# Cluster attention and two soft mixtures on one core: small TensorE products padded to the whole array, centroid products moved behind the product with v

## Chip, cores, metric

One core of a Trainium2 chip runs one program. The metric is the device time in microseconds (us) of one execution; the kernel before takes 589.06 us in the median of three runs (588.84 to 589.12).

## What is computed

The program chains three blocks; the change lies in the first. For 2 x 8 heads of 768 positions and 64 channels:

```python
q_assign = argmax(q_n @ c_n.T)            # 16 centroids per head, q and c normalised
k_assign = argmax(k_n @ c_n.T)
mask = q_assign[:, None] == k_assign[None, :]
scores = where(mask, scale * q @ k.T, -1e9)
attn = softmax(scores)                     # sum + 1e-9
x = attn @ v                               # (1536, 512) over the heads
h = x @ w_in                               # 512 -> 2048, f64 words decoded on the chip
g = P(h) / (Q(h) + 1e-6)
x = g @ w_out                              # 2048 -> 512
out = soft_moe(x, phi, w1, w2)             # logits = x @ phi, 32 slots
```

`w_out @ phi` is formed ahead of time (the tile `wphi0`), so that the logits can be had straight from g.

## The kernel before

**Attention** works on eight pairs of heads. A pair takes twelve slots; slot n (n from 0 to 95, k = n % 12, loop at line 692) computes one 128-row tile of transposed scores for both heads (`a2_mm`, lines 458 and 459), its exponential on ScalarE (`a2_exp`, 463), and the product with v of the slot before (`a2_av`, 472). In the same slot, ten slots ahead (`LEAD`), runs the pass that finds row maxima and sums: `a1_mm` (383, 384) on TensorE, the negated copy with the row minimum on VectorE (`a1_neg`, 393), the exponential with the row sum on ScalarE (`a1_exp`, 401). Two PSUM tiles (`psS`) are shared: `a2_mm` waits for `a2_exp`, `a1_mm` for `a1_neg` of the slot before. `a1_neg` also follows `a1_exp` of the slot before, since both use the tile `nv`.

**Side work** is put into the slots by hand. A plan holds, for a slot, lists by engine; the order of PE, ACT, DVE and POOL is the order written (`manual_schedule`). A slot issues the lists S, A, D0, D, D1, D2, G0, G (DMA; ScalarE; VectorE; GpSimd), then `a2_mm`, `a2_exp`, `a2_av` of the slot before, `a1_exp`, `a1_mm`, `a1_neg`, and last the list P of TensorE (739). Three kinds of side work exist.

- `prep(p)` (236) readies a later pair, from k = 8 on, over 18 slots: two groups of centroid products (`scores`, 251, at k = 9 and 10), scaling (`scaled`, 256), transposes (`scT`, 266), the argmax on VectorE (`best`, `first`), one-hot transposes (`ohT`, 293, k = 3), their copy with row counts on ScalarE (`count`, 296, k = 4), the mask weights (`masks`, 304, k = 6), two products `nonhot` (309, k = 6), four products `alive` (322, k = 8 to 11), and GpSimd's splits of q and k into parts (260 to 335).
- `stats` (403) turns sums into a bias that enters the scores: GpSimd steps (419 to 432, k = 8 and 2 or a slot later), two transposes `rows` (437, k = 10 and 4) and two VectorE multiplies `place` (444, k = 11 and 5).
- `decode_steps` (551) turns the f64 words of w_in and w_out into floats: VectorE (563, 564, 570, 574), ScalarE (567), GpSimd (579, 586, 587). For w_out, `wphi_steps` (595) adds transposes (601), a product with phi (610), a copy (617), and after each fourth block transposes (622) and a reduction (625). One decode starts every third slot, from slot 72 on every second.

All small TensorE results go to a ring of three PSUM tiles (`m_tile`, 167), so a small product also waits until the reader of the third tile back is done. TensorE products here have these array shapes: scores of `a1` and `a2` and all f32 transposes use 128 columns and 80 or 128 rows; `scores` 64 rows x 32 columns, `alive` 64 x 128, `nonhot` 64 x 64, `ohT` 128 x 64, `rows` and the phi product 128 x 32, the product with v 128 x 64.

After attention (from about 335 us) come `h_mm` and the mixtures; the change doesn't touch them.

Of the kernel before, what the change touches and what calls it, by code (L numbers as in the profile page):

```python
# [8 lines left out]
F32 = mybir.dt.float32  # L9
F32R = mybir.dt.float32r  # L10
BF16 = mybir.dt.bfloat16
# [26 lines left out]
def shape_constants():  # L38
    c = np.zeros((128, C_END), np.float32)
    p = np.arange(128)  # L40
    c[p, C_ID + p] = 1.0
    c[:, C_SUM:C_SUM + 128] = p[:, None] % 32 == p[None, :] % 32
    c[0:32, C_SGN] = 1.0
    c[32:64, C_SGN] = -BIG

    for i in range(3):
        c[96 + 6 * i:99 + 6 * i, C_STAT + i] = 1.0
        c[99 + 6 * i:102 + 6 * i, C_STAT + i] = -1.0
    b = np.zeros((128, B_END), np.float32)
    b[p, B_ID + p] = 1.0  # L50

    b[0:16, B_MASK:B_MASK + 128] = 1.0
    b[16:32, B_MASK + 128:B_MASK + 256] = 1.0
    b[0:16, B_MASK + 256:B_MASK + 272] = 1.0
    b[16:32, B_MASK + 272:B_MASK + 288] = 1.0
    for i in range(64):
        b[i, B_ADD + 256 + i] = -1.0 if i < 32 else 1.0
    b[:, B_RANK:B_RANK + 16] = 16.0 - np.arange(16)
    return c, (b.view(np.uint32) >> 16).astype(np.uint16)
# [3 lines left out]
def tile_kernel(ctx, tc, qT, kT, v, cenT, cenP, consts, constsb, ab, w_in, w_out, phi, w1, w2, out, dbg=None):  # L63
# [22 lines left out]
    def xs_tile(dt, name):  # L86
# [42 lines left out]
    OPENW = 4  # L129
    ops = [[{n: att.tile([128, S], F32R, name=f"{n}_{i}_{h}") for n in ("q1", "q2", "k1", "k2")}  # L130
            for h in range(2)] for i in range(NBUF)]
    stat = [att.tile([128, 2, 32], BF16, name=f"stat{i}") for i in range(2)]
    for t in stat:
        POOL.memset(t, 0.0)

    def fill(i):
        for h in range(2):
# [34 lines left out]
    def first_pair(r, o, f):  # L172

        hold = f["hold"]

        def nonhot_k(h):
            m = psS.tile([128, 2, 512], F32, tag="S", name="s1")
            for c in range(2):
                PE.matmul(m[64:80, c, 0:HS], hold["W"][:, 288 + 16 * h:304 + 16 * h],
                          hold["oT"][:, c * HS:(c + 1) * HS], start=True, stop=True)  # L180
            ACT.activation(o[h]["k2"][64:80, :].rearrange("p (c n) -> p c n", c=2), m[64:80, :, 0:HS], AF.Copy, scale=-BIG)

        def nonhot_q(h, c):
            m = m_tile()
            w = slice(c * HS, (c + 1) * HS)
            PE.matmul(m[64:80, 0:HS], hold["W"][:, 256 + 16 * h:272 + 16 * h], hold["oT"][:, w], start=True, stop=True)
            ACT.copy(o[h]["q2"][64:80, w], m[64:80, 0:HS])

        def q0(h):
            w = slice(0, HS)  # L190
            q1, q2 = o[h]["q1"], o[h]["q2"]
            qa = hold.pop(("qa", h, 0))
            ACT.copy(q1[:, w], qa)
            POOL.tensor_scalar(q2[0:64, w], qa[0:64, :], 1.0, 1.0, ALU.mult, ALU.mult)
            DVE.tensor_tensor(q1[64:128, w], qa[64:128, :], q1[64:128, w].bitcast(F32), ALU.subtract)

        def front():
            f["scores"](0)
# [12 lines left out]
            idle(12)  # L211
            f["ohT"]()
            f["count"]()
            idle(8)
            f["masks"]()

        def back():
            f["alive"](0, 0)
            f["alive"](1, 0)
            f["qalive"](0, 0)  # L220
            f["qalive"](1, 0)
            nonhot_k(0)
            q0(0)
            nonhot_q(0, 0)
            q0(1)
            nonhot_k(1)
            nonhot_q(1, 0)
            idle(4)

        rest = [(0, "P", lambda: (f["alive"](0, 1), f["alive"](1, 1))),  # L230
                (1, "D", lambda: (f["qalive"](0, 1), f["qalive"](1, 1))),
                (1, "G", lambda: (f["qsplit"](0, 1), f["qsplit"](1, 1))),
                (1, "P", lambda: (nonhot_q(0, 1), nonhot_q(1, 1)))]
        return front, back, rest

    def prep(p):
# [52 lines left out]

        def ohT():  # L290
            m = hold["mo"] = m_tile(BF16)
            for i in range(6):
                PE.transpose(m[0:64, i * 128:(i + 1) * 128], hold["oh"][:, i].rearrange("p g c -> p (g c)"), identb)

        def count():
            ACT.activation(tile_(t_p, "oT", [64, S], BF16), hold.pop("mo")[0:64, 0:S], AF.Identity,
                           accum_out=tile_(s2_p, "cnt", [64, 1], F32))

        def masks():

            pres = tile_(s2_p, "pres", [64, 1], F32)
            DVE.memset(pres, 0.0)
            DVE.tensor_scalar(pres[0:32, :], hold["cnt"][32:64, :], 1.0, None, ALU.min)
            DVE.scalar_tensor_tensor(tile_(s2_p, "W", [64, B_ADD - B_MASK], BF16), cb[0:64, B_MASK:B_ADD], pres,
                                     cb[0:64, B_ADD:B_RANK], ALU.mult, ALU.add)

        def nonhot(c):
            m = hold["m", c] = m_tile()
            PE.matmul(m[0:64, 0:HS], hold["W"][:, 256:320], hold["oT"][:, c * HS:(c + 1) * HS], start=True, stop=True)

        def signed(c):
            nh = hold["nh"] if c else tile_(t_p, "nh", [64, S], F32R)
# [24 lines left out]
        if p == 0:  # L337
            return first_pair(r, o, locals())
        return [
            (1, "P", lambda: scores(0)),  # L340
            (2, "P", lambda: scores(1)),
            (3, "A", lambda: scaled(0)),
            (3, "P", lambda: scT(0)),
            (4, "A", lambda: scaled(1)),
# [58 lines left out]
    def stats(p, half):  # L403
# [8 lines left out]
        def parts(a):  # L412

            nv, ssum = nvs[p, half]
            l = hold["l"]
            st = stat[half][:, :, 0:18].rearrange("p h (i k r) -> p k h i r", i=3, k=2)
            val = nv.rearrange("p k (h i) -> p k h i", h=2)
            if a == 0:
                POOL.tensor_scalar(hold["s"], ssum, 1e-9, 1.0, ALU.add, ALU.mult)
# [13 lines left out]

        def rows():
            hold["m"] = m_tile(BF16)
            for h in range(2):
                PE.transpose(hold["m"][96:128, h * 128:(h + 1) * 128], stat[half][:, h, :], identb)

        def place():

            m = hold["m"]
            own = cst[96:128, C_STAT:C_END].unsqueeze(2).to_broadcast([32, 3, 128])
            for h in range(2):
                DVE.tensor_tensor(ops[p % NBUF][h]["q2"][96:128, half * HS:(half + 1) * HS].rearrange("p (i t) -> p i t", i=3),
                                  m[96:128, h * 128:(h + 1) * 128].unsqueeze(1).to_broadcast([32, 3, 128]), own, ALU.mult)

        return [(0, "A", log)] + [(0, "G0", lambda a=a: parts(a)) for a in range(6)] + [(1, "P", rows), (2, "D0", place)]

# [141 lines left out]
        return [(-3, "S", dma), (0, "D1", bits), (1, "A", expo), (1, "D1", mant), (2, "D1", sign),  # L590
                (3, "G0", value)] + (after(hold) if after else [(4, "G", parts)])

    wph = {}

    def wphi_steps(f):

        def steps(hold):
            def tr():
                m = hold["m"] = m_tile()
                for c in range(NCC):  # L600
                    PE.transpose(m[:, c * 128:(c + 1) * 128], hold["w"][:, c * 128:(c + 1) * 128], ident)

            def tcopy():
                hold["wT"] = dec_p.tile([128, 512], F32, tag="wT", name="wT")
                ACT.copy(hold["wT"], hold.pop("m"))

            def mm():
                m = hold["m"] = m_tile()
                for c in range(NCC):
                    PE.matmul(m[32 * c:32 * c + 32, 0:128], ph[:, c, :], hold["wT"][:, c * 128:(c + 1) * 128],  # L610
                              start=True, stop=True)

            def keep_():
                k = f % 4
                if k == 0:
                    wph["t"] = dec_p.tile([128, 512], F32, tag="wph", name="wph")
                DVE.tensor_copy(wph["t"][:, k * 128:(k + 1) * 128], hold.pop("m")[:, 0:128])

            def fin():
                m = hold["m"] = m_tile()  # L620
                for k in range(4):
                    PE.transpose(m[:, k * 128:(k + 1) * 128], wph["t"][:, k * 128:(k + 1) * 128], ident)

            def total():
                DVE.tensor_reduce(wphi0[:, f - 3:f + 1, :], hold.pop("m").rearrange("p (k c s) -> p k s c", k=4, c=4),
                                  AX.X, ALU.add)

            return [(4, "P", tr), (5, "A", tcopy), (5, "P", mm), (6, "D1", keep_)] + \
                ([(6, "P", fin), (7, "D1", total)] if f % 4 == 3 else [])
        return steps  # L630

    w_in_w = w_in.bitcast(I32)
# [59 lines left out]
    for n in range(-LEAD, NSL + 1):  # L692
# [25 lines left out]
        if n > 0:  # L718
            pp, pk = divmod(n - 1, 12)
            a2_av(pp, pk)  # L720
            if pk % 6 == 5:
                copy, split = a2_x(pp, pk // 6)
                copy()
                if n < NSL:
                    add(n + (1 if k else 2), [(0, "G", split)])
                else:
                    split()
# [465 lines left out]
```

## Time and profile before

| | |
|---|---|
| median of three runs | 589.06 us |
| span of the profiled execution, first to last instruction | 588.3 us |
| what the median holds beside that span | 0.8 us |
| busy in the span: PE, DVE, ACT, POOL | 553.0, 462.1, 392.4, 375.0 us |
| attention's slots 0 to 95 | 41 to 335 us |
| granted TensorE clock | 1.00 of full speed throughout attention |

Busy times of TensorE include pipelining, so 94% of the span doesn't mean that it never waits. L458 is line 458 of the kernel before. In a timeline a row is start, duration, engine, line, operation, output<-inputs, shapes, count and, in brackets, the idle time before it and what ended it; in the chain of waits a row is start, duration, engine, output and line.

### The profile page before, as it was taken

How to read it: one execution, taken by the hardware profiler on the slowest of the kernel's cores; microseconds unless marked ns; L12 is line 12 of the kernel's file. 1: busy time of each engine (PE TensorE's matmuls, PEld its weight loads, DVE VectorE, ACT ScalarE, POOL GpSimd, SP SyncE). 2: the span in 40 equal slices, each digit the busy share in tenths (PEclk: the TensorE clock that was granted, in tenths of full speed). 3: DMA queues.
4: the chain of work that ended last, by engine and by line, in shares of the span. 5: the costliest groups of instructions: out<-in, count | busy, mean ns of one | idle time of the engine just before them, and what ended most of it. 6: DMA issues, size and time to landing. Idle time of an engine off the chain costs nothing.

```text
span 588.3 us, 9927 instructions
## 1 busy us (share of the span) xinstructions
PE 553.0 (94%) x3345; PEld 343.3 (58%) x3348; DVE 462.1 (79%) x817; ACT 392.4 (67%) x713; POOL 375.0 (64%) x487
## 2 busy tenths in 40 slices
PE   8899999999999999999899999999999999988995
PEld 3455555565555555555555587777577767743363
DVE  5789788798788896888996179999989998971033
ACT  3577777677677776877777478878678876750111
POOL 8759899697996997979668375565456654611000
PEclk9999999999999999999999999999999999999999
DMA  8613553353434542333342476775476665379996
GB/s 224 218 60 118 166 195 125 115 197 139 143 117 166 197 150 91 114 132 124 128 159 90 144 247 222 269 251 211 159 283 229 227 230 191 121 321 364 421 418 255
DMA packets 37906, 113.77 MB, mean 193 GB/s; under 512 B 5216, under 2 KB 5664, under 8 KB 33248
## 3 DMA queue, kind: packets, MB, share of 16 engines
q1 hardware_dynamic: 37856, 113.14, 54.6%
q8 instruction: 26, 0.43, 0.3%
q14 instruction: 24, 0.20, 0.1%
HBM read 96.02 MB, written 15.73 MB: 190 GB/s over the span
## 4 chain that ended last, share of the span: by engine, by line
PE 56%; DVE 23%; ACT 8%; issue 6%; POOL 5%; DMA 2%; SPq 0%; DVEq 0%; POOLq 0%; ACTq 0%
PE h L809 6%; PE h L810 5%; PE h L812 5%; PE s L383 5%; DVE neg L393 5%; PE av L472 4%; PE s L458 4%; PE s L384 3%; PE s L459 3%; PE pb L1044 3%; PE pb L1115 3%; DVE mh L564 2%; ACT neg L401 2%; PE gt L870 2%; ACT e L463 2%
## 5 line engine op out<-in xcount | busy, mean ns | idle before, releaser
L393 DVE TENSOR_SCALAR_CACHE_REDUCE neg<-s 128x768 f32<-128x768 f32 x96 | 91.2, 952 | 36.6 <-ACT neg L401 25.7
L463 ACT ACTIVATE e<-s 128x768 f32<-128x768 f32 x96 | 77.5, 807 | 58.4 <-PE s L459 58.3
L401 ACT ACTIVATE neg<-neg,nv 128x768 f32<-128x768 f32 x96 | 89.5, 932 | 9.5 <-DVE neg L393 9.3
L383 PE MATMUL s<-k,q 128*128 128x384 f32 x192 | 75.7, 394 | 13.0 <-DVE neg L393 9.2
L840 POOL TENSOR_SCALAR q<-u,babs 128x512 f32<-128x512 f32 x47 | 39.6, 844 | 70.5 <-ACT u L838 70.5
L472 PE MATMUL av<-e,vt 128*64 128x384 f32 x384 | 83.2, 511 | 0.2 <-ACT e L463 0.2
L809 PE MATMUL h<-xh,w 128*128 128x512 f32 x192 | 80.6, 420 | 0.0
L383 PEld LDWEIGHTS s<-k,q 128*128 128x128 f32 x192 | 36.2, 189 | 68.1 <-DVE neg L393 27.4
L810 PE MATMUL h<-xl,w 128*128 128x512 f32 x192 | 75.9, 395 | 0.0
L458 PE MATMUL s<-q,k 128*128 128x384 f32 x192 | 73.2, 381 | 0.7 <-DVE neg L393 0.6
L842 POOL TENSOR_TENSOR q<-q,u 128x512 f32<-128x512 f32 x47 | 62.8, 1337 | 3.9
L384 PE MATMUL s<-k,q 80*128 80x384 f32 x192 | 65.0, 339 | 0.0
L459 PE MATMUL s<-q,k 128*128 128x384 f32 x192 | 64.7, 337 | 0.0
L812 PE MATMUL h<-xh,w 128*128 128x512 f32 x192 | 52.6, 396 | 0.0
L579 POOL TENSOR_TENSOR w<-mh,ex 128x512 f32<-128x512 f32 x32 | 44.1, 1378 | 10.8 <-DMA w_out<-w 5.4
L809 PEld LDWEIGHTS h<-xh,w 128*128 128x128 f32 x192 | 36.2, 189 | 16.1 <-issue 1.9
L458 PEld LDWEIGHTS s<-q,k 128*128 128x128 f32 x192 | 36.0, 188 | 16.2 <-issue 8.1
L849 ACT ACTIVATE r<-q,epsc 128x512 f32<-128x512 f32 (+1 forms) x49 | 33.5, 685 | 17.0 <-POOL q L842 16.4
L859 DVE SCALAR_TENSOR_TENSOR p<-q,p 128x512 f32<-128x512 f32 (+1 forms) x49 | 44.0, 901 | 0.1
L841 DVE TENSOR_TENSOR p<-p,h 128x512 f32<-128x512 f32 x47 | 31.8, 677 | 15.5 <-ACT p L839 15.4
L838 ACT ACTIVATE u<-h 128x512 f32<-128x512 f32 x47 | 27.8, 591 | 24.1 <-PE h L812 24.1
L812 PEld LDWEIGHTS h<-xh,w 128*128 128x128 f32 x192 | 36.3, 189 | 8.9
(193 smaller groups left out, 1215.6 us busy)
## 6 DMA issues: line engine op xcount, KB each, us to landing
wt<-w SPq DMA_DIRECT2D x32, 1024.0 KB, 8.3
w<-w_in SPq DMA_DIRECT2D x96, 256.0 KB, 3.3
raw<-w_in SPq DMA_DIRECT2D x16, 512.0 KB, 3.7
raw<-w_out SPq DMA_DIRECT2D x16, 512.0 KB, 3.3
w_in<-w SPq DMA_DIRECT2D x16, 512.0 KB, 2.7
rawk<-kT SPq DMA_DIRECT2D x14, 384.0 KB, 4.0
rawq<-qT SPq DMA_DIRECT2D x14, 384.0 KB, 3.4
w_out<-w SPq DMA_DIRECT2D x16, 256.0 KB, 3.4
```

Source lines behind the costliest of these rows:

```text
L383: PE.matmul(ps[:, c, 0:HS], o["q1"][:, it], o["k1"][:, w], start=True, stop=False)
L384: PE.matmul(ps[:, c, 0:HS], o["q2"][0:80, it], o["k2"][0:80, w], start=False, stop=True)
L393: DVE.tensor_scalar(neg, s1s.pop((p, idx))[:, :, 0:HS], -1.0, None, ALU.mult, ALU.min, accum_out=nvs[p, half][0][:, 0, col:col + 1])
L401: ACT.activation(neg, neg, AF.Exp, scale=-1.0, bias=nv[:, 0, col:col + 1], accum_out=ssum[:, col:col + 1])
L458: PE.matmul(ps[:, h, 0:HS], o["k1"][:, jt], o["q1"][:, w], start=True, stop=False)
L459: PE.matmul(ps[:, h, 0:HS], o["k2"][:, jt], o["q2"][:, w], start=False, stop=True)
L463: ACT.activation(e, s2s.pop((p, k))[:, :, 0:HS], AF.Exp)
L472: PE.matmul(a[64 * h:64 * h + 64, 0:HS], vs[p][:, h, j, :], e[:, h, :], start=(j == 0), stop=(j == 5))
L809: PE.matmul(h, wh[:, c, :], xh[t][:, c, :], start=(c == 0), stop=False)
L810: PE.matmul(h, wh[:, c, :], xl[t][:, c, :], start=False, stop=False)
L812: PE.matmul(h, wl[:, c, :], xh[t][:, c, :], start=False, stop=(c == NCC - 1))
L842: POOL.tensor_tensor(q, q, u, ALU.mult)
```

## The change

1. The weights `W` and the one-hot tile `oT` become fixed tiles with zero rows up to 80 (and zero columns up to 128 for `nonhot`), so that `alive` and `nonhot` use 80 rows and 128 columns. The zeros are written once by GpSimd at the start.
2. `ohT` makes three transposes of 128 columns in place of six of 64; `count` then needs two ScalarE copies of 384 columns in place of one of 768, and `masks` adds two counts.
3. `rows` makes one transpose of a 128-column tile in place of two of 32; `place` reads one head's rows at partition 0, the other's at 96.
4. The phi product is turned round: the decoded block is the stationary operand (128 x 128), phi the moving one (32 columns), and the four parts add up in PSUM. The transposes of line 622 and the reduction of line 625 go; the copy is 32 columns wide.
5. The two `scores` groups of `prep` move from list P into a new list T, issued behind `a2_av`, ahead of `a1_mm`.

```diff
-        c[96 + 6 * i:99 + 6 * i, C_STAT + i] = 1.0
-        c[99 + 6 * i:102 + 6 * i, C_STAT + i] = -1.0
+        for r in range(0, 128, 32):
+            c[r + 6 * i:r + 3 + 6 * i, C_STAT + i] = 1.0
+            c[r + 3 + 6 * i:r + 6 + 6 * i, C_STAT + i] = -1.0
...
-    stat = [att.tile([128, 2, 32], BF16, name=f"stat{i}") for i in range(2)]
+    stat = [att.tile([128, 4, 32], BF16, name=f"stat{i}") for i in range(2)]
+    Ws = [att.tile([96, 384], BF16, name=f"W{i}") for i in range(2)]
+    oTs = att.tile([96, S], BF16, name="oT")
...
+    for t in Ws:
+        POOL.memset(t[0:64, 320:384], 0.0)
+        POOL.memset(t[64:96, :], 0.0)
+    POOL.memset(oTs[64:96, :], 0.0)
...
-            for i in range(6):
-                PE.transpose(m[0:64, i * 128:(i + 1) * 128], hold["oh"][:, i].rearrange("p g c -> p (g c)"), identb)
+            for j in range(3):
+                PE.transpose(m[:, j * 128:(j + 1) * 128],
+                             hold["oh"][:, 2 * j:2 * j + 2].rearrange("p i g c -> p (i g c)"), identb)
...
-            ACT.activation(tile_(t_p, "oT", [64, S], BF16), hold.pop("mo")[0:64, 0:S], AF.Identity,
-                           accum_out=tile_(s2_p, "cnt", [64, 1], F32))
+            m, o = hold.pop("mo"), oTs[0:64, :].rearrange("p (j r t) -> p r j t", j=3, r=2)
+            hold["oT"] = oTs[0:80, :]
+            cnt = tile_(s2_p, "cnt", [64, 2], F32)
+            for i in range(2):
+                ACT.activation(o[:, i], m[64 * i:64 * i + 64, 0:HS].rearrange("p (j t) -> p j t", j=3), AF.Identity,
+                               accum_out=cnt[:, i:i + 1])
...
-            DVE.tensor_scalar(pres[0:32, :], hold["cnt"][32:64, :], 1.0, None, ALU.min)
+            DVE.tensor_scalar(pres[0:32, :], hold["cnt"][32:64, 0:1], hold["cnt"][32:64, 1:2], 1.0, ALU.add, ALU.min)
+            hold["W"] = Ws[p % 2][0:80, :]
...
-            PE.matmul(m[0:64, 0:HS], hold["W"][:, 256:320], hold["oT"][:, c * HS:(c + 1) * HS], start=True, stop=True)
+            PE.matmul(m[:, 0:HS], hold["W"][:, 256:384], hold["oT"][:, c * HS:(c + 1) * HS], start=True, stop=True)
...
-            (1, "P", lambda: scores(0)),
-            (2, "P", lambda: scores(1)),
+            (1, "T", lambda: scores(0)),
+            (2, "T", lambda: scores(1)),
...
-            for h in range(2):
-                PE.transpose(hold["m"][96:128, h * 128:(h + 1) * 128], stat[half][:, h, :], identb)
+            PE.transpose(hold["m"][:, 0:128], stat[half].rearrange("p b r -> p (b r)"), identb)
...
-                    PE.matmul(m[32 * c:32 * c + 32, 0:128], ph[:, c, :], hold["wT"][:, c * 128:(c + 1) * 128],
-                              start=True, stop=True)
+                    PE.matmul(m[:, 0:NS], hold["wT"][:, c * 128:(c + 1) * 128], ph[:, c, :],
+                              start=(c == 0), stop=(c == NCC - 1))
...
-                DVE.tensor_copy(wph["t"][:, k * 128:(k + 1) * 128], hold.pop("m")[:, 0:128])
-            def fin():
...
-            def total():
...
+                DVE.tensor_copy(wphi0[:, f, :], hold.pop("m")[:, 0:NS])
...
             a2_av(pp, pk)
+        run(n, "T")
+        if n > 0:
             if pk % 6 == 5:
```

## Rows read from the trace of the kernel before

**Rows 1.** Windows: two periods of twelve slots, k = 2 to k = 2; busy (count) by engine.
```profile
85.04:123.99 38.95, 36.91 (x210) 21.34 (x208) 33.10 (x61) 29.17 (x54) 32.65 (x47) 1.00 0.45 155
123.99:162.94 38.95, 37.36 (x213) 21.82 (x212) 33.25 (x62) 29.28 (x54) 32.65 (x47) 1.00 0.44 146
```
**Rows 2.** Who waited for whom, POOL: us in total, times, longest.
```profile
POOL s L419 <- ACT neg L401: 19.9, 8, 3.4
```
**Rows 3.** Timeline of POOL, slots 17 to 19 (first of the two periods).
```profile
95.93 1.84 POOL L261 TENSOR_TENSOR k<-rawk,k 64x768 fp32r<-64x768 f32 x1
...
100.23 1.75 POOL L579 TENSOR_TENSOR w<-mh,ex 128x512 f32<-128x512 f32 x1
```
**Rows 4.** Timeline of DVE, the same stretch.
```profile
96.61 1.71 DVE L574 SCALAR_TENSOR_TENSOR ex<-raw,ex 128x512 int32<-128x512 int32 x1
98.35 0.96 DVE L393 TENSOR_SCALAR_CACHE_REDUCE neg<-s 128x768 f32<-128x768 f32 x1
...
100.76 1.50 DVE L564 TENSOR_SCALAR mh<-raw 128x512 int32<-128x512 int32 x1
```
**Rows 5.** Timeline of DVE, slots 28 and 29 (second period).
```profile
131.41 0.68 DVE L625 TENSOR_REDUCE wphi<-mf 128x128 f32<-128x512 f32 x1
...
136.00 1.26 DVE L574 SCALAR_TENSOR_TENSOR ex<-raw,ex 128x512 int32<-128x512 int32 x1
137.30 0.96 DVE L393 TENSOR_SCALAR_CACHE_REDUCE neg<-s 128x768 f32<-128x768 f32 x1
```
**Rows 6.** All runs of two lines: duration ns min/median/max, first and last start.
```profile
L564 DVE TENSOR_SCALAR mh<-raw x32: 415/726/1505, 43.2 to 317.2; 128x512 int32<-128x512 int32 x32
...
L574 DVE SCALAR_TENSOR_TENSOR ex<-raw,ex x32: 676/806/1710, 50.5 to 318.5; 128x512 int32<-128x512 int32 x32
```
**Rows 7.** Chain of waits, second period: start, duration, what.
```profile
130.31 0.44 PE mf L622 x4
130.75 0.45 PE mb L293 x6
131.20 0.38 PE s L458
...
133.81 0.21 PE mb L437 x2
...
143.11 0.44 PE mf L601 x4
143.55 0.18 PE s L458
...
145.95 0.36 PE mf L610 x8
146.31 0.27 PE mf L322
...
149.44 0.78 PE mf L251 x8
```
**Rows 8.** All runs of line 1031 on PE: min/median/max ns, first and last start.
```profile
L1031 PE MATMUL pb<-cst,sin x8: 276/276/297, 539.6 to 540.4; 128*128 128x32 f32 x8
```
**Rows 9.** ACT groups: busy us, mean ns, idle before.
```profile
L483 ACT COPY x<-av 128x384 f32<-128x384 f32 x16 | 7.7, 479 | 1.0 <-PE av L472 1.0
L296 ACT ACTIVATE oT<-mb 64x768 bf16<-64x768 bf16 x8 | 6.4, 795 | 6.0 <-PE mb L293 6.0
...
L296 ACT ACTIVATION_READ_ACCUMULATOR oT<-mb 64x1 f32 x8 | 1.5, 190 | 0.0
```
**Rows 10.** Timeline of ACT, slot 23 (k = 11): the second `scaled`.
```profile
117.92 0.57 ACT L256 ACTIVATE sc<-mf,pc 128x384 f32<-128x384 f32 x1
```
**Rows 11.** Timeline of POOL at the start.
```profile
1.56 0.73 POOL L143 MEMSET q<- 32x768 f32 x1
...
11.28 0.83 POOL L260 TENSOR_SCALAR k<-rawk 128x768 fp32r<-128x768 f32 x1 [0.84 <-POOL k L145]
...
18.39 0.98 POOL L194 TENSOR_SCALAR q<-qa 64x384 fp32r<-64x384 f32 x2 [1.42 <-DVE qa L326]
```

More of the change, by code (lines that the diff above doesn't have):

```diff
@@ L178, in nonhot_k @@
             for c in range(2):
-                PE.matmul(m[64:80, c, 0:HS], hold["W"][:, 288 + 16 * h:304 + 16 * h],
-                          hold["oT"][:, c * HS:(c + 1) * HS], start=True, stop=True)
+                PE.matmul(m[64:80, c, 0:HS], hold["W"][0:64, 288 + 16 * h:304 + 16 * h],
+                          hold["oT"][0:64, c * HS:(c + 1) * HS], start=True, stop=True)
             ACT.activation(o[h]["k2"][64:80, :].rearrange("p (c n) -> p c n", c=2), m[64:80, :, 0:HS], AF.Copy, scale=-BIG)
@@ L185, in nonhot_q @@
             w = slice(c * HS, (c + 1) * HS)
-            PE.matmul(m[64:80, 0:HS], hold["W"][:, 256 + 16 * h:272 + 16 * h], hold["oT"][:, w], start=True, stop=True)
+            PE.matmul(m[64:80, 0:HS], hold["W"][0:64, 256 + 16 * h:272 + 16 * h], hold["oT"][0:64, w], start=True, stop=True)
             ACT.copy(o[h]["q2"][64:80, w], m[64:80, 0:HS])
@@ L302, in masks @@
             DVE.memset(pres, 0.0)
-            DVE.tensor_scalar(pres[0:32, :], hold["cnt"][32:64, :], 1.0, None, ALU.min)
-            DVE.scalar_tensor_tensor(tile_(s2_p, "W", [64, B_ADD - B_MASK], BF16), cb[0:64, B_MASK:B_ADD], pres,
+            DVE.tensor_scalar(pres[0:32, :], hold["cnt"][32:64, 0:1], hold["cnt"][32:64, 1:2], 1.0, ALU.add, ALU.min)
+            hold["W"] = Ws[p % 2][0:80, :]
+            DVE.scalar_tensor_tensor(Ws[p % 2][0:64, 0:B_ADD - B_MASK], cb[0:64, B_MASK:B_ADD], pres,
                                      cb[0:64, B_ADD:B_RANK], ALU.mult, ALU.add)
@@ L415, in parts @@
             l = hold["l"]
-            st = stat[half][:, :, 0:18].rearrange("p h (i k r) -> p k h i r", i=3, k=2)
+            st = stat[half][:, 0:4:3, 0:18].rearrange("p h (i k r) -> p k h i r", i=3, k=2)
             val = nv.rearrange("p k (h i) -> p k h i", h=2)
@@ L435, in rows @@
             hold["m"] = m_tile(BF16)
-            for h in range(2):
-                PE.transpose(hold["m"][96:128, h * 128:(h + 1) * 128], stat[half][:, h, :], identb)
+            PE.transpose(hold["m"][:, 0:128], stat[half].rearrange("p b r -> p (b r)"), identb)
         def place():
             m = hold["m"]
-            own = cst[96:128, C_STAT:C_END].unsqueeze(2).to_broadcast([32, 3, 128])
             for h in range(2):
+                rows = slice(96 * h, 96 * h + 32)
+                own = cst[rows, C_STAT:C_END].unsqueeze(2).to_broadcast([32, 3, 128])
                 DVE.tensor_tensor(ops[p % NBUF][h]["q2"][96:128, half * HS:(half + 1) * HS].rearrange("p (i t) -> p i t", i=3),
-                                  m[96:128, h * 128:(h + 1) * 128].unsqueeze(1).to_broadcast([32, 3, 128]), own, ALU.mult)
+                                  m[rows, 0:128].unsqueeze(1).to_broadcast([32, 3, 128]), own, ALU.mult)
         return [(0, "A", log)] + [(0, "G0", lambda a=a: parts(a)) for a in range(6)] + [(1, "P", rows), (2, "D0", place)]
@@ L591, in decode_steps @@
                 (3, "G0", value)] + (after(hold) if after else [(4, "G", parts)])
-    wph = {}
     def wphi_steps(f):
@@ L609, in mm @@
                 for c in range(NCC):
-                    PE.matmul(m[32 * c:32 * c + 32, 0:128], ph[:, c, :], hold["wT"][:, c * 128:(c + 1) * 128],
-                              start=True, stop=True)
+                    PE.matmul(m[:, 0:NS], hold["wT"][:, c * 128:(c + 1) * 128], ph[:, c, :],
+                              start=(c == 0), stop=(c == NCC - 1))
             def keep_():
-                k = f % 4
-                if k == 0:
-                    wph["t"] = dec_p.tile([128, 512], F32, tag="wph", name="wph")
-                DVE.tensor_copy(wph["t"][:, k * 128:(k + 1) * 128], hold.pop("m")[:, 0:128])
-            def fin():
-                m = hold["m"] = m_tile()
-                for k in range(4):
-                    PE.transpose(m[:, k * 128:(k + 1) * 128], wph["t"][:, k * 128:(k + 1) * 128], ident)
-            def total():
[L625 to L629, printed above, removed]
+                DVE.tensor_copy(wphi0[:, f, :], hold.pop("m")[:, 0:NS])
+            return [(4, "P", tr), (5, "A", tcopy), (5, "P", mm), (6, "D1", keep_)]
         return steps
```

## The prediction

> **What bounds the kernel now.** I read the windows first. A period of twelve slots takes 38.95 us, of which TensorE is busy about 95% [rows 1]. That looks like a kernel held by TensorE, and then every saving on TensorE would come out of the time. But the two windows differ: the second holds the transposes of line 622, PE's busy time is 0.45 us higher, and it is as long to the hundredth [rows 1]. TensorE had room for 0.45 us, so something else sets the length.
>
> The list of POOL's waits shows what. POOL has only one large wait in a period, of up to 3.4 us, at the first step of `stats` (line 419), which needs the row sums of `a1_exp` [rows 2]. For the rest of the period it works back to back. VectorE is tied to it in turn: its decode operations stay busy until the operation on POOL ends. Line 574 starts at 96.61, takes 1.71 us and ends at 98.32, while POOL's line 261 runs to 97.77; line 564 starts at 100.76 and ends at 102.26, POOL's line 579 at 101.98 [rows 3, 4]. Undisturbed they take 0.676 and 0.415 us [rows 6]. The next `a1_neg` stands behind them, `a1_mm` of the next slot behind that, and so on to the `a1_exp` for which POOL waits at line 419. That is a loop: POOL's run of work, then VectorE let go, `a1_neg`, `a1_mm`, the decoded block's transposes, ScalarE's queue, `a1_exp`, `stats`, POOL again. No step of the last part is edited.
>
> The second period shows what this loop does with a delay. There line 625 adds 0.68 us to VectorE and line 574 starts 12.01 us into the period instead of 11.57. It then takes only 1.26 us, and `a1_neg` starts at 137.30, which is 13.31 us into the period. In the first it starts at 98.35, also 13.31 [rows 1, 4, 5]. A delay of 0.44 us ahead of POOL's release point has vanished. An advance there should vanish in the same way.
>
> **The change part by part, on TensorE.** All lengths of TensorE work in a period are from the chain [rows 7], where one step's length includes draining the one before. A score product of 384 columns takes 0.18 us behind the same shape and 0.38 behind another, so leaving and re-entering the common shape costs 0.20.
>
> - The phi product (k = 2 and 8) takes 0.36 for its eight records today. Turned round, it is four products with 128 x 128 f32 stationary and 32 moving columns. Line 1031 has that very form: eight records from 539.6 to 540.4, so about 0.11 us each [rows 8]. Eight records make 0.89. The stationary load isn't hidden behind 32 columns. At k = 2: 0.36 + 0.20 becomes 0.89, **+0.33**. At k = 8, with one `alive` (0.27, then 0.18 as a score product of the same columns): 0.36 + 0.27 + 0.20 becomes 0.89 + 0.18, **+0.24**.
> - `ohT`, 0.45 + 0.20, becomes three transposes: 0.23 as half of today's six, 0.33 by line 601's 0.11 each; I take 0.27. **-0.38**.
> - `rows` at k = 4, 0.21 + 0.20, becomes one transpose, 0.10: **-0.31**.
> - `nonhot`, 0.27 + 0.18 + 0.20, becomes 2 x 0.18: **-0.30**.
> - `alive` at k = 11: 0.27 + 0.20 becomes 0.18, **-0.29**. At k = 9 and 10 there is a `scores` group too. It stays 0.78 behind the product with v, but the 0.20 goes, since that product changes the shape anyway: 0.27 + 0.78 + 0.20 becomes 0.18 + 0.78, **-0.29**; with `rows` at k = 10, 1.46 becomes 0.18 + 0.10 + 0.78, **-0.40**.
>
> The sum is -1.40 us in a period. The transposes of line 622 (0.44) go from every second, which makes about -1.62 on average. There are five full periods, so TensorE alone would get about **8.1 us** back.
>
> On the array's shape a rule speaks against one part. The Trainium skill, page "TensorEngine Tiling (Array Packing)", section "When to Use Tiling", advises for a moving side of 32 or less to swap the operands and tile by columns. That is the phi product as it was, and the rows above (0.36 against 0.89) agree with it for the product alone.
>
> **What becomes of it.** Ahead of POOL's release point the net effect is a loss. At k = 2, 0.33 us is added ahead of `a2_mm` of k = 3. `count` on ScalarE (k = 4) goes from one activation of 768 columns and its read, 0.795 + 0.190, to two of 384 (0.479, a copy of that size) with two reads: 2 x 0.669 - 0.985 = +0.35 [rows 9]. Both stand ahead of `a1_exp` of k = 4, so of the next `a1_neg`: up to 0.68 us later. `ohT` and `rows` give back 0.69 on TensorE, but behind the place where ScalarE is late. Line 574's stretch in the first period is 1.71 - 0.68 = 1.03 us, which covers 0.68 as the second period covered its 0.44; then comes line 564's own stretch. Price of this part: 0, and 0.68 where the cover is missing.
>
> From k = 9 to 11 TensorE gains 0.98 us. The move of `scores` puts a wait in its place. There are three tiles in the PSUM ring. With the second `scores` group issued ahead of k = 10's list P, the ring's order shifts by one, and the second `alive` product of k = 11 takes the tile whose reader is the second `scaled`. That one stands on ScalarE in list A of the next slot, behind the exponentials of this one; it ran at 117.92 for 0.57 us, until 118.49 [rows 10], when the next period's slot 0 was about to begin. A TensorE that comes there earlier by the 0.29 and 0.40 of k = 9 and 10 waits for about those 0.7 us. Behind that wait on TensorE's queue stand slot 0's scores, and slot 0 begins about when it did. The ring wait of `rows` on the first `scaled` costs nothing, since that one is done a slot earlier. No step is moved on the queues of SP or POOL, and no DMA moves.
>
> The zeroing at the start adds 1792 columns on POOL (two of 64, two of 384, one of 768, and 128 of `stat`). At 0.73 us for 768 [rows 11] that is 1.7 us, between 0.9 (bf16 at half the time) and 3 with issue. POOL waits 0.84 at line 260 and 1.42 at line 194 later [rows 11], 2.26 in all. So I take 0; uncovered it is 0.7, and new collisions with VectorE make it 1 us either way. `count` costs another 0.35 or less in the first pairs. The mask step's second operand and the rows read at partition 0: 0, hidden behind the 0.96 of `a1_neg`.
>
> In the tail (slots 72 to 95) side work is decode only. Two reductions of line 625 (0.68 each) and two sets of transposes go, the narrower copy saves about 0.1 each, and every phi product is 0.5 longer on TensorE. I take -0.3, between -0.7 and +0.4.
>
> **Sum.** Periods 0, start 0, tail -0.3: 588.3 + 0.8 - 0.3 = **588.8 us**. The profiled execution is 588.3 plus 0.8 around its span, 589.1, the median of the runs itself. The forecast's own range is 587.3 to 590.3. A measurement of this kernel can tell some 0.2%, 1.2 us, from no change.
>
> **Rivals.**
>
> *TensorE sets the end after all.* POOL's loop also passes over `a1_mm`, and if the loop's slack on TensorE is an accident of these two windows, some or all of the 8.1 us comes back: 581, or 585 for half. For it: 95% busy. Against it: the equal periods [rows 1, 5]. Chance 0.20.
>
> *The 0.68 us isn't absorbed, and it gets slower.* Place: the path from k = 2 over ScalarE's queue to `a1_neg` of k = 5. Price: 0.68 us in three periods, and 0.24 in the two in which line 625 (0.44 of delay) goes: 3 x 0.68 + 2 x 0.24 = 2.5 us, 591.6. It decides where line 574's stretch is under 0.68 us. The median of line 574 is 0.806 against 0.676 at least [rows 6], so most are hardly stretched; but those at k = 5, the two that I looked at, are. Chance 0.18.
>
> On this a page goes further. The Trainium skill, page "SBUF — State Buffer", section "Who interferes with whom", says that VectorE and GpSimd share a port pair under an exclusive lock. The stretched rows agree (1.50 against 0.415 us). By it a small delay could let the other engine in first, which costs a whole operation instead of a fraction.
>
> *The change doesn't do what it says.* The zero rows might not join the shapes, since `a1_mm`'s own parts and the f32 transposes still alternate beside bf16 products, and the 0.20 steps stay. Then TensorE keeps its length, and the time is 589 too. Chance 0.04.
>
> **How the numbers follow.** The forecast has 0.58: of that 0.42 within 0.2% of 589.06, 0.10 faster, 0.06 slower, from its own range. The first rival adds 0.20 to faster, the second 0.18 to slower, the third 0.04 to the same. Faster 0.30, same 0.46, slower 0.24. For 8 in 10 the range reaches to the upper half of the first rival (584.8) and to the second's price (591.6).
>
> **What would show it.** Right: periods stay 38.95 us between the same slots; PE's busy time falls by 1 us or more while its idle time grows; the phi product's group takes about 0.89; the second `alive` at k = 11 waits for ScalarE; line 574 at k = 5 is shorter and `a1_neg` still 13.31 us into the period; POOL's wait at line 419 stays at about 3.4. Wrong for the first rival: periods near 37.3, and POOL's run of work with gaps or its wait at `stats` shorter. Wrong for the second: periods near 39.4 with `a1_neg` later than 13.31 and POOL's wait longer.

## The result and the profile after

The changed kernel takes 596.1 us (median of four runs, 594.9 to 596.26), the kernel before 589.09 beside it: a ratio of 1.010, interval 1.0082 to 1.0117. It is 7 us slower, and the forecast was 588.8. The profiled execution after has a span of 593.1 and a time of 594.9, the shortest of the four. A run's time is 1.8 us above its span here and in every later run that shows both, so the profiled execution of before, with its span of 588.3, probably took about 590.1, 1 us more than its median, and the 0.8 us that the prediction put beside that span is too small.

The windows show first where the time went: the four periods from slot 14 to slot 62, k = 2 to k = 2 (start:end, length, then busy time and count of PE, PEld, DVE, ACT and POOL, granted clock, DMA share, GB/s).

```profile
83.75:123.23 39.48, 35.83 (x205) 22.59 (x203) 34.45 (x61) 29.38 (x56) 33.18 (x47) 1.00 0.44 145
123.23:163.76 40.53, 38.59 (x204) 24.70 (x203) 31.54 (x61) 29.16 (x56) 32.38 (x47) 0.92 0.44 147
163.76:204.29 40.53, 38.60 (x204) 24.70 (x203) 31.69 (x61) 29.16 (x56) 32.17 (x47) 0.92 0.44 141
204.29:244.38 40.09, 37.17 (x204) 23.28 (x203) 32.90 (x61) 29.29 (x56) 33.94 (x49) 0.96 0.41 136
```

The same four periods take 155.71 us in the kernel before (85.04 to 240.75; two of them are [rows 1]) and 160.63 here, 4.92 more. Two losses can be told apart. The first period, at a full clock, is 0.53 longer than before. The others are longer by 1.3 to 1.6, and there the granted clock is below 1.00, which it never is between these slots in the kernel before. At slot 14 the kernel was still 1.29 us ahead, at slot 95 it is 5.86 behind: 1.29 gained at the start, 4.92 lost in the periods, 2.23 lost behind them.

**The first loss** begins at k = 9. Timeline of DVE after, slots 21 and 22 (start, duration, operation, idle before and what ended it):

```profile
111.20 0.96 DVE L406 TENSOR_SCALAR_CACHE_REDUCE neg<-s 128x768 f32<-128x768 f32 x1 [1.91 <-PE s L397]
...
112.55 1.56 DVE L583 SCALAR_TENSOR_TENSOR mh<-raw,mh 128x512 f32<-128x512 uint32 x1
114.57 0.96 DVE L406 TENSOR_SCALAR_CACHE_REDUCE neg<-s 128x768 f32<-128x768 f32 x1 [0.46 <-PE mb L449]
```

The same operations before (L393 is `a1_neg`, L570 the decode operation that is L583 after):

```profile
110.35 0.96 DVE L393 TENSOR_SCALAR_CACHE_REDUCE neg<-s 128x768 f32<-128x768 f32 x1 [0.89 <-ACT neg L401]
...
111.70 0.89 DVE L570 SCALAR_TENSOR_TENSOR mh<-raw,mh 128x512 f32<-128x512 uint32 x1
114.00 0.96 DVE L393 TENSOR_SCALAR_CACHE_REDUCE neg<-s 128x768 f32<-128x768 f32 x1 [1.41 <-ACT neg L401]
```

`a1_neg` is 0.85 us later, and the bracket names another releaser: before it was the exponential of the slot before, now it is TensorE, whose `a1_mm` stands behind the moved `scores` group. The decode operation behind it is 0.85 later too and meets the next operation of POOL. POOL in the same stretch, after:

```profile
112.29 1.27 POOL L600 TENSOR_TENSOR w<-w,w 128x512 fp32r<-128x512 f32 x1
113.54 0.95 POOL L346 TENSOR_SCALAR q<-qa 128x384 fp32r<-128x384 f32 x1
...
117.20 1.55 POOL L348 TENSOR_TENSOR q<-qa,q 64x384 fp32r<-64x384 f32 x1
118.83 1.29 POOL L592 TENSOR_TENSOR w<-mh,ex 128x512 f32<-128x512 f32 x1
```

The same operations before (L587 is L600 after, L333 is L346, L335 is L348, L579 is L592):

```profile
112.13 1.59 POOL L587 TENSOR_TENSOR w<-w,w 128x512 fp32r<-128x512 f32 x1
113.70 0.50 POOL L333 TENSOR_SCALAR q<-qa 128x384 fp32r<-128x384 f32 x1
...
116.91 1.33 POOL L335 TENSOR_TENSOR q<-qa,q 64x384 fp32r<-64x384 f32 x1
118.31 1.29 POOL L579 TENSOR_TENSOR w<-mh,ex 128x512 f32<-128x512 f32 x1
```

Line 583 runs until 114.11, and line 346 takes 0.95 where it took 0.50. POOL, 0.10 us ahead at slot 17, is 0.52 behind when line 592 starts, and the next `stats` and `a1_neg` inherit that. The 0.62 is the sum of four rows: 0.27 more at `stats` of k = 8 (line 436, 0.46 where it took 0.19), 0.32 less at line 600, 0.45 more at line 346 and 0.22 more at line 348. The last three, 0.35 together, stand behind the late `a1_neg`. The first is not the move's: the run without the move (no_T, below) has the same 0.46 there.

**The second loss** is at k = 2. Timeline of PE after, slot 26 (L621 is the phi product):

```profile
124.10 0.87 PE L485 MATMUL av<-e,vt 128*64 128x384 f32 x4
126.80 0.44 PE L396 MATMUL s<-k,q 128*128 128x384 f32 x1 [1.83 <-DMA rawq<-qT]
...
127.68 1.75 PE L621 MATMUL mf<-ph,wT 128*128 128x32 f32 x8
```

The DMA named is not what it waited for: `a1_neg` of the slot before ends at 126.73. Before, the wait at this place was 0.65. TensorE now comes 0.76 earlier (slot 26 starts at 123.23, not 123.99) and `a1_neg` 0.42 later (125.79, not 125.37): 0.65 + 0.76 + 0.42 = 1.83. The same stretch in windows of 1 us:

```profile
125.00:126.00 1.00, 0.00 (x0) 0.00 (x0) 1.00 (x2) 0.08 (x1) 1.00 (x2) 1.00 0.07 27
...
127.00:128.00 1.00, 1.00 (x7) 1.00 (x6) 1.00 (x2) 0.97 (x3) 0.91 (x2) 0.76 0.69 266
128.00:129.00 1.00, 1.00 (x6) 1.00 (x7) 1.00 (x2) 0.35 (x2) 0.92 (x2) 0.50 0.00 0
...
133.00:134.00 1.00, 1.00 (x6) 0.70 (x6) 0.00 (x0) 0.24 (x1) 1.00 (x1) 0.50 0.00 0
134.00:135.00 1.00, 1.00 (x7) 0.79 (x4) 0.95 (x3) 0.69 (x3) 0.92 (x3) 0.83 0.00 0
```

TensorE stands idle, then the granted clock falls from 1.00 to 0.50 (2.4 to 1.2 GHz) at about 127.5 and stays there until about 134.2. In that time the phi product takes 1.75 us instead of the 0.97 that it takes at the full clock, the `a1_neg` at 134.05 waits 3.01 us for TensorE, and POOL's wait at `stats` grows from 3.4 to 4.3. The Trainium skill, page "TensorE: Matmul & The Clock Gate", section "Terms", speaks of a monitor that watches TensorE's activity and gates its clock; what it does here is in these rows.

The clock does not fall behind every such wait. At slot 14, too, TensorE waits 1.83, and the first period runs at 1.00 throughout:

```profile
87.32 0.44 PE L396 MATMUL s<-k,q 128*128 128x384 f32 x1 [1.83 <-DVE neg L406]
```

The same 1.83 stands at slots 14, 26, 38, 50 and 62. Behind slots 26, 38 and 50 the half clock follows, for some 6.7, 6.7 and 3.4 us; behind slots 14 and 62 it doesn't. The three other executions of the changed kernel have a lower mean clock (0.975 to 0.977, against 0.982 in the profiled one) and take 1.1 to 1.4 us more.

### The profile page after: what moved, and what is told of

It is laid out like the page before. It is cut to its first block, busy times and chain, and to the rows that moved or that the text cites. A ratio compares the mean times of both kernels' runs of the same rounds, so it can differ in the third digit from the quotient of the medians.

```text
span 593.1 us, 9824 instructions
## 1 busy us (share of the span) xinstructions
PE 550.5 (93%) x3292; PEld 357.0 (60%) x3292; DVE 459.7 (78%) x813; ACT 394.2 (66%) x729; POOL 378.7 (64%) x492
## 4 chain that ended last, share of the span: by engine, by line
PE 53%; DVE 24%; POOL 7%; ACT 6%; issue 5%; DMA 4%; SPq 1%; DVEq 0%; POOLq 0%; ACTq 0%
PE av L485 6%; PE s L396 6%; DVE neg L406 5%; PE h L809 4%; PE s L397 4%; PE s L471 4%; PE h L812 3%; PE h L810 3%; PE s L472 3%; PE pb L1115 3%; PE pb L1044 2%; DVE p L858 2%; PE mf L621 2%; PE mf L258 2%; DVE p L859 2%
## 5 line engine op out<-in xcount | busy, mean ns | idle before, releaser
L396 PE MATMUL s<-k,q 128*128 128x384 f32 x192 | 77.2, 402 | 18.3 <-DVE neg L406 14.3
L485 PE MATMUL av<-e,vt 128*64 128x384 f32 x384 | 85.2, 523 | 0.2 <-ACT e L476 0.2
L396 PEld LDWEIGHTS s<-k,q 128*128 128x128 f32 x192 | 37.2, 194 | 76.1 <-DVE neg L406 41.1
L471 PE MATMUL s<-q,k 128*128 128x384 f32 x192 | 75.1, 391 | 1.3 <-DVE neg L406 0.8
L397 PE MATMUL s<-k,q 80*128 80x384 f32 x192 | 66.3, 345 | 0.0
L472 PE MATMUL s<-q,k 128*128 128x384 f32 x192 | 66.0, 344 | 0.0
L592 POOL TENSOR_TENSOR w<-mh,ex 128x512 f32<-128x512 f32 x32 | 42.7, 1336 | 12.3 <-DMA w_out<-w 5.5
L859 DVE SCALAR_TENSOR_TENSOR p<-q,p 128x512 f32<-128x512 f32 (+1 forms) x49 | 45.5, 933 | 0.1
L471 PEld LDWEIGHTS s<-q,k 128*128 128x128 f32 x192 | 37.7, 196 | 4.8 <-issue 2.4
```

The source lines that it names most:

```text
L396: PE.matmul(ps[:, c, 0:HS], o["q1"][:, it], o["k1"][:, w], start=True, stop=False)
L397: PE.matmul(ps[:, c, 0:HS], o["q2"][0:80, it], o["k2"][0:80, w], start=False, stop=True)
L471: PE.matmul(ps[:, h, 0:HS], o["k1"][:, jt], o["q1"][:, w], start=True, stop=False)
L472: PE.matmul(ps[:, h, 0:HS], o["k2"][:, jt], o["q2"][:, w], start=False, stop=True)
L485: PE.matmul(a[64 * h:64 * h + 64, 0:HS], vs[p][:, h, j, :], e[:, h, :], start=(j == 0), stop=(j == 5))
```

## The experiments

Theory T: the move of the `scores` groups ahead of `a1_mm` makes `a1_neg` late, which costs POOL half a us a period; and the longer wait at k = 2 costs clock. Theory P: the longer phi product is what costs. The table has the four periods from slot 14 to 62 of each profiled run, the start of slots 8 and 95, and the times; the ratio is to the kernel before beside it. The three columns on the left are those of one profiled execution each, which stood 2.4 us above the run's median in no_T, 2.0 above it in T_only and 1.6 below it in phi_only.

| run | four periods | slot 8 | slot 95 | median | ratio (interval) |
|---|---|---|---|---|---|
| before | 155.71 | 65.41 | 332.80 | 589.09 | 1 |
| after | 160.63 | 64.78 | 338.66 | 596.10 | 1.010 (1.0082 to 1.0117) |
| no_T | 156.28 | 64.07 | 335.57 | 590.55 | 1.001 (0.9986 to 1.0033) |
| T_only | 157.27 | 67.42 | 337.00 | 592.27 | 1.0056 (1.0035 to 1.0077) |
| old_phi | 157.98 | 63.81 | 336.59 | 593.76 | 1.0067 (1.0046 to 1.0088) |
| warm | 161.46 | 65.56 | 341.11 | 600.03 | 1.0187 (1.0133 to 1.024) |
| warm2 | 158.21 | 64.05 | 335.68 | 593.78 | 1.0072 (1.0049 to 1.0094) |
| parts123 | 156.81 | 62.95 | 334.79 | 591.23 | 1.0028 (1.0013 to 1.0042) |
| phi_only | 156.66 | 65.14 | 334.52 | 591.82 | 1.0028 (1.0012 to 1.0045) |
| light | 152.04 | 67.68 | 329.39 | 586.69 | 0.995 (0.9935 to 0.9966) |
| l2 | 152.04 | 65.27 | 327.27 | 582.89 | 0.9898 (0.9855 to 0.9941) |
| l2_after | 151.98 | 63.73 | 325.74 | 580.62 | 0.9852 (0.9818 to 0.9886) |
| l2_no_T | 150.52 | 62.95 | 322.98 | 578.58 | 0.9819 (0.9785 to 0.9853) |
| l2_pad | 150.26 | 62.94 | 322.11 | 579.54 | 0.9828 (0.9789 to 0.9866) |

**no_T**, the change without the move:

```diff
-            (1, "T", lambda: scores(0)),
-            (2, "T", lambda: scores(1)),
+            (1, "P", lambda: scores(0)),
+            (2, "P", lambda: scores(1)),
```

> The changed kernel with the two centroid groups back in list P, behind a1_mm; all else of the change stays. Theory T (the move of the groups puts 0.78 us ahead of a1_mm at k = 9 and 10, so a1_neg comes up to 0.85 us later, line 583 on VectorE meets another GpSimd operation, and GpSimd loses 0.5 us a period): a1_neg of slots 21 and 22 no longer late, GpSimd's run 38.95 us a period as before, time 589 if TensorE's clock holds, up to 592 if TensorE still stands long enough at k = 2 (about 1.5 us) for the clock to fall. Rival theory P (the phi product of 0.89 us is what delays the loop): the move is innocent, 595 to 596 as now.

It measured 590.55, and cannot be told from the kernel before. A period is 39.07 us, 0.14 over before's mean of 38.93. Windows of its first two periods:

```profile
83.53:122.61 39.08, 36.07 (x204) 22.60 (x203) 33.56 (x61) 29.38 (x56) 32.79 (x47) 1.00 0.45 148
122.61:161.69 39.08, 36.07 (x205) 22.61 (x203) 33.59 (x61) 29.38 (x56) 32.79 (x47) 1.00 0.45 152
```

PE's busy time is down by about 1.1 us and the length isn't. The clock holds here; its longest wait between slots 8 and 72 is 0.9. It falls in the tail instead, between 277 and 282 and between 291 and 295, the first time behind a wait of 1.98 at slot 73 (timeline of its PE):

```profile
276.60 0.44 PE L396 MATMUL s<-k,q 128*128 128x384 f32 x1 [1.98 <-DVE neg L406]
```

So theory P falls for the whole change: without the move it is about as fast as before.

**T_only**, the kernel before with the move alone (in the loop over slots, and "P" to "T" for both groups):

```diff
             a2_av(pp, pk)
+        run(n, "T")
+        if n > 0:
             if pk % 6 == 5:
```

> The kernel before with the move of the two centroid groups alone. Theory T: a1_neg at k = 9 and 10 is 0.6 to 0.9 us late, GpSimd loses 0.5 us in each of five periods, 591 to 592, without a fall of the clock in attention if TensorE's wait at k = 2 stays under about 1.3 us. Theory P: 589, no change.

592.27: slower, as T has it, and 0.3 above its range. Its four periods are 39.30 to 39.33 us, 0.39 longer and not 0.5, at a full clock, and at k = 9 the same picture stands. Timeline of its DVE:

```profile
113.51 0.96 DVE L393 TENSOR_SCALAR_CACHE_REDUCE neg<-s 128x768 f32<-128x768 f32 x1 [1.67 <-PE s L384]
...
114.86 1.49 DVE L570 SCALAR_TENSOR_TENSOR mh<-raw,mh 128x512 f32<-128x512 uint32 x1
```

Timeline of its POOL:

```profile
115.78 0.95 POOL L333 TENSOR_SCALAR q<-qa 128x384 fp32r<-128x384 f32 x1
...
121.14 1.28 POOL L579 TENSOR_TENSOR w<-mh,ex 128x512 f32<-128x512 f32 x1 [0.69 <-DVE ex L574]
```

TensorE releases `a1_neg`, the decode operation takes 1.49, and POOL's line 333 takes 0.95. The last row shows where the move's cost ends up: line 579 needs what line 574 makes, VectorE is late with it, and POOL waits 0.69. It does so in each of the four periods; between the same slots the kernel before and no_T have no such wait. The profiled execution is also 2.0 us late at slot 8 already, which wasn't followed up.

**old_phi**, the changed kernel with the phi product as before:

```diff
-                    PE.matmul(m[:, 0:NS], hold["wT"][:, c * 128:(c + 1) * 128], ph[:, c, :],
-                              start=(c == 0), stop=(c == NCC - 1))
+                    PE.matmul(m[32 * c:32 * c + 32, 0:128], ph[:, c, :], hold["wT"][:, c * 128:(c + 1) * 128],
+                              start=True, stop=True)
```

with `keep_`, `fin` and `total` as before.

> The changed kernel with the phi product as before (eight tiled records, the transposes of line 622 and the reduction of line 625 back); the move stays. Theory T: GpSimd's 0.5 us a period stays lost; the wait of about 1.8 us at k = 2 stays, and the clock still falls behind it, but the product that follows costs about 0.7 instead of 1.75 us at the low clock: 592 to 595. Theory P: 589.

593.76, inside T's range. Its waits reach 1.8 us and the clock still falls in three of the four periods (0.96 each), so the low clock doesn't hang on the 32-column product. With the short product the four periods are 2.65 us less than the changed kernel's.

**warm** and **warm2** put products with a zero stationary operand behind the product with v at k = 2, so that TensorE doesn't stand idle; they add nothing to `av`. The number is 4 and 2 rounds (16 and 8 records):

```diff
+    cold = att.tile([128, 64], F32, name="cold")
+    DVE.memset(cold, 0.0)
...
+        if 0 < 12 * p + k + 1 < 72 and (k + 1) % 12 in (2,):
+            for _ in range(2):
+                for h in range(2):
+                    PE.matmul(a[64 * h:64 * h + 64, 0:HS], cold, e[:, h, :], start=False, stop=False)
```

> The changed kernel with sixteen records of the product with v more at k = 2 of slots 2 to 62, with a zero stationary operand that adds nothing, right where TensorE waits 1.8 us for a1_neg. If the wait is what lowers the clock: granted clock 1.00 from slot 0 to 95, periods of 39.5 us, three periods 1.0 us shorter, 592.5 to 593.5. If the clock falls for another reason (the 32-column phi product behind the wait, for one): half clock still shows in slots 26, 38 and 50, 596.

> As warm, but with eight zero records at k = 2 in place of sixteen. The sixteen took 2.7 us, 0.9 more than the wait that they were to fill, so that run kept the clock at 1.00 and lengthened the period itself. Eight take about 1.4 of the 1.83 us. If the wait lowers the clock: 1.00 from slot 0 to 95, periods of 39.4 to 39.6 us, 592.5 to 593.5. If a product of that shape had to replace the whole wait, or the clock falls for another reason: half clock shows again in slots 26, 38 and 50, 595 to 597.

warm missed its time by far, 600.03, since the records took longer than the wait that they filled (the whole group, and what comes behind it):

```profile
127.81 2.75 PE L492 MATMUL av<-e,cold 128*64 128x384 f32 x16
130.50 0.44 PE L398 MATMUL s<-k,q 128*128 128x384 f32 x1
...
131.31 0.97 PE L627 MATMUL mf<-ph,wT 128*128 128x32 f32 x8
```

From slot 0 to 95 of the profiled execution (598.1) the clock stayed at 1.00, and the phi product took 0.97. Two of the other three executions, at 601.95 and 603.01, have a lower mean clock (0.987 and 0.984), and where it fell in them wasn't recorded. warm2 is the cleaner one; its median is 0.3 above its range. Windows of its second and third periods, those at 0.92 in the changed kernel:

```profile
123.95:163.51 39.56, 37.17 (x212) 23.16 (x211) 34.57 (x61) 29.45 (x56) 32.66 (x47) 1.00 0.44 147
163.51:203.07 39.56, 37.20 (x213) 23.18 (x211) 34.55 (x61) 29.44 (x56) 32.65 (x47) 1.00 0.44 148
```

39.56 in place of 40.53, with more work on TensorE. So the idle time at this place is what brings the clock down: filled with work, the place shows no fall at slots 14 to 62 of warm2, against three of five in the changed kernel and four of five in old_phi. The length of the wait alone doesn't settle it: 1.83 at slot 14 was not followed by a fall, and in light (below) half clock stands from 63.5 to 67 though the longest wait shortly before it, at 61.67, is 1.06. What else decides wasn't found. By the difference to warm2 the low clock costs 160.63 - 158.21 = 2.4 of the 4.92 us. The other 2.5 are there at a full clock: the move's 1.56 (T_only) and the rest's 0.57 (no_T) make 2.13, and 0.4 stay open.

**parts123** is no_T with old_phi's edit, the padding alone. **phi_only** is the kernel before with the product turned round alone.

> The changed kernel without the move of the centroid groups and with the phi product as before: only the padding of alive and nonhot, the three-column-block ohT and the single rows transpose are left. Theory T (the move costs GpSimd's 0.4 to 0.5 us a period, and a longer wait of TensorE at k = 2 costs clock): GpSimd's run stays 38.95 to 39.1 us a period, TensorE's savings vanish in its waits, the start keeps the gain of 1.0 to 1.5 us that the changed kernel, no_T and old_phi all have at slot 0 to 8: 587.5 to 588.5 where the clock holds. Theory P (padding is harmless, the phi product is the cost): 587.5 to 588.5 too, but then no_T should have been slow, which it wasn't; so this run prices the padding alone.

> The kernel before with the phi product turned round and nothing else. Theory T: a2_mm of k = 3 and 9 is 0.3 to 0.5 us later and the delay ends in VectorE's stretched operations, periods 38.95 to 39.1, tail within 0.5: 588.5 to 590. Theory P: GpSimd's run 39.3 or more a period, 591 or more.

Both expectations were too low: 591.23 and 591.82. Each part, which alone should have vanished in the stretch of VectorE's operations, costs 0.24 to 0.27 us a period (39.20 and 39.17). POOL's rows of the first period show where. From the start of the line 261 that runs into slot 14 to the end of POOL's wait at line 419 it is 23.36 us before, 23.30 in parts123 and 23.50 in phi_only. So parts123 loses its 0.27 behind that wait (by before's line numbers, one line 334 takes 1.02 where it took 0.50, and the line 335 behind it 0.32 less), and phi_only a good half of its 0.24 ahead of it. In parts123 the clock falls again at slots 62 and 73. In phi_only it holds throughout attention, TensorE is busy 37.66 of a period's 39.17 us, and the run is slower all the same.

**light** and **l2** test the bound itself. One of POOL's operations, the second rounded copy in `qsplit`, goes to ScalarE; in light for all pairs, in l2 for pairs 2 to 7:

```diff
+        def qsame(h, c):
+            ACT.copy(o[h]["q2"][0:64, c * HS:(c + 1) * HS], hold["qa", h, c][0:64, :])
...
             POOL.tensor_scalar(q1[:, w], qa, 1.0, 1.0, ALU.mult, ALU.mult)
-            POOL.tensor_scalar(q2[0:64, w], qa[0:64, :], 1.0, 1.0, ALU.mult, ALU.mult)
+            if p < 2:
+                POOL.tensor_scalar(q2[0:64, w], qa[0:64, :], 1.0, 1.0, ALU.mult, ALU.mult)
...
-        ]
+        ] + [(14 + i, "A", lambda i=i: qsame(i % 2, i // 2)) for i in range(4 if p > 1 else 0)]
```

> The kernel before with one of GpSimd's operations moved: the second rounded copy of the q halves (four of 0.5 to 0.8 us a period) is made on ScalarE at the head of the slot. If GpSimd's run of work sets the period: 38.95 less 1 to 2.3 us a period until TensorE's own sum stops it (about 37.3 us), 580 to 585. If TensorE sets the end: 588 to 590, or slower by ScalarE's delay of a2_exp.

> The kernel before with GpSimd's second rounded copy of the q halves on ScalarE for pairs 2 to 7 only; the two first pairs keep it on GpSimd, since the run that moved it there too lost 2.3 us by slot 8. GpSimd-bound theory: the periods keep what that run had (37.6 to 38.4 us), the start is as before, 584 to 585.5. If the copy's place was not what cost the start: 586 to 587 as that run.

light gains 0.5%, at 586.69 short of its range, since its start is 2.3 us late; l2 gains 1.0%, which is below its range in time. With no edit on TensorE at all, a period goes from 38.93 to 38.01. POOL's run of work did set it, in the main: POOL is busy 2.1 us less in a period, of which 0.92 arrives, and POOL's wait at `stats` grows from 12.6 to 14.6 us over the four periods. VectorE, too, is busy 2.2 us less in a period, and what is due to it alone wasn't tried apart. In l2 TensorE is busy 147.80 of the four periods' 152.04 us, and its waits for `a1_neg` between slots 14 and 62 are 0.8 us instead of 3.8. Who waited for whom there (us in total, times, longest):

```profile
PE mf L251 <- ACT sc L256: 2.0, 4, 0.5
PE mf L309 <- DVE W L304: 1.4, 2, 0.7
PE s L387 <- DVE neg L397: 0.8, 2, 0.4
```

**l2_after**, **l2_no_T** and **l2_pad** are after, no_T and parts123 with l2's edit.

> The changed kernel with the same move of GpSimd's copies. If GpSimd's run is what swallowed the change's savings, most of the 1.4 to 1.6 us a period on TensorE arrives once GpSimd has 2 us less to do: periods 36.5 to 37.3, k = 2's wait under 1 us and no low clock behind it, 580 to 584, faster than the kernel before with that move alone. If the change's order costs by itself (the groups ahead of a1_mm), no faster than the kernel before with that move: 584 to 588.

> As the run with the whole change, with the centroid groups in list P. GpSimd-bound theory with the move as the harmful part: 36.5 to 37.2 us a period, 578 to 583, at or below the run with the whole change. If the move is worth its 0.2 us a group once GpSimd is not the bound: 1 to 2 us above it.

> As the run without the move, with the phi product as before too: padding alone. TensorE has 0.35 us a period less to do than with the phi product turned round (0.57 at the two products, less 0.22 for the transposes of line 622): 1 to 2 us below the run without the move if TensorE sets the period there, the same if it doesn't.

All three beat both kernels; l2_no_T is the best median, 578.58, 1.8% below the kernel before. But l2_after came into its range for another reason than the one given: its four periods are l2's (151.98 and 152.04), and the 1.5 us that it leads at slot 95 it has from the start. TensorE waits for `a1_neg` again; who waited for whom, from 64 to 274 us (total, times, longest; in l2 it is 0.8 there):

```profile
PE s L400 <- DVE neg L410: 8.4, 15, 0.9
```

Without the move (l2_no_T) the periods are 37.63 us, 0.38 shorter than in l2 and not the 36.5 to 37.2 that were expected. More than half of its lead on l2, 4.29 us at slot 95, is there at slot 8 already (2.32). l2_pad's periods are the same as l2_no_T's within 0.1 us, so the turned product costs next to nothing there: of the two branches of that expectation, "the same" came.

## Why the prediction was wrong

**What bounds the kernel** was read rightly in the main. POOL's run holds the period (l2), and savings on TensorE vanish in it: no_T has about 1.1 us less TensorE work in a period and none of it in the time.

**The delay ahead of POOL's release point** (0.33 for the phi product, 0.35 for `count`) was absorbed as argued, up to that point. In the changed kernel's first period `a2_exp` of k = 4 is 0.57 later than before, `a1_neg` of slot 18 starts at 98.25, against 98.35 in [rows 4], and line 587 takes 1.68 where it took 1.71. Counted from TensorE's slot 14, as the prediction's sign has it, that `a1_neg` stands 14.50 us into the period and not 13.31; but that is because TensorE begins the period 1.29 earlier and POOL only 0.10, so the sign couldn't tell. no_T has both delays, and its periods are 0.14 longer, not the 0.68 and 0.24 of the slower rival. So that rival had the right side by the wrong mechanism. With one delay alone it is less clear: phi_only has lost 0.14 by POOL's release point, but T_only, without that delay, has lost 0.12 there too.

**The step that failed**, under the sum's term "Periods 0" (measured 4.92 us over four), is the one on k = 9 to 11: "The move of `scores` puts a wait in its place." It priced the move as a wait in the PSUM ring, behind TensorE alone. That wait didn't come: TensorE ran the second `alive` at 116.92 without waiting. What was left out is that list T stands ahead of `a1_mm`, so that 0.78 us of other work now stands in front of `a1_neg`, and VectorE's decode operations stand behind that on its queue. I had argued that a delay in front of POOL's release point vanishes, and didn't ask what a delay of 0.85 does in the other half of the period, where VectorE's decode operation starts in between POOL's operations. There, in the changed kernel's first period, it adds 0.45 and 0.22 us at two of POOL's operations and takes 0.32 from a third; in T_only it makes POOL wait 0.69 for line 574, and the period is 0.39 longer. On this the Trainium skill, page "SBUF — State Buffer", section "Who interferes with whom", goes on that the order of issue decides who blocks. The rows agree: line 583 starts while line 600 runs and is stretched (1.56), then line 346 starts while line 583 runs and is stretched in its turn (0.95).

**The second failed step** is what a wait of TensorE costs. The forecast let TensorE's idle time grow for nothing, and no rival had the clock in it. Waits of 1.8 us at one place brought it to half in three of the four periods, for some 6.7, 6.7 and 3.4 us, which cost 2.4 us in all by warm2. The evidence was there in part: the place already had TensorE's wait of 0.65, and the change sent TensorE there 0.76 earlier.

**Sizes.** The phi product was sized rightly (0.89; 0.97 with its drain). As groups of a timeline, drain included, `ohT` takes 0.34 (in warm; 0.52 before) and `rows` 0.23 (0.28 before). TensorE's busy time in the first period is 1.33 below the mean of before (35.83 against 37.16), where the sum had about 1.62. The slips in the sum are small: `nonhot` is -0.29 by its own terms, and the rivals' times count from 589.1 while the forecast is 588.8. The padding and the turned product, taken at 0 in a period, cost 0.24 to 0.27 each when alone. The tail from slot 72 on, taken at -0.3, lost 1.8 (2.2 from slot 62 on), at a full clock and behind waits of 1.97 and 1.87 us at slots 73 and 77; the cause wasn't sought. The start, taken at 0, gained 0.6 by slot 8, and 1.3 to 2.5 in no_T, old_phi and parts123. All of these have the padding; what in it gives the start its gain wasn't tried apart. The zeroing did delay POOL there, line 260 from 11.28 to 12.42; the "bf16 at half the time" of its lower bound isn't so, since the memset of 768 bf16 columns takes 0.74 and that of 768 f32 columns 0.73. Behind attention the clock falls near 540 us in some profiled executions, the one of before among them, and not in others, the changed kernel's among them. By an estimate that is about 1 us: the changed kernel is 5.86 behind at slot 95 and 4.8 at the end. That wasn't followed up either.

## What to carry to other kernels

When work is moved ahead of an instruction, follow that instruction's reader and what stands behind the reader on its queue, over the whole period: here 0.78 us on an engine that wasn't the bound came out as 0.4 us a period on the one that was. A saving on an engine that isn't the bound becomes a wait, and on TensorE a wait that was harmless can bring the clock down; so shorten the bound first (moving one POOL copy gave 1.0%), and add the savings then (1.8% in all without the move, more than half of the further gain from the start).

## What was not expected of the hardware

VectorE and POOL stretch each other in both directions: POOL's line 346 takes 0.51 us undisturbed and 0.95 beside line 583, and line 583 takes 1.56 beside line 600, where the same operation took 0.89 in the kernel before. The three parts' costs don't add: the padding alone costs 0.27 us a period, the phi product alone 0.24, both together (no_T) 0.14. And with eight zero records more in its idle time TensorE did more work in less time (39.56 against 40.53 us a period), while the same wait of 1.83 us left the clock alone at two of its five places.
